# Reordering the start, the sums of x and the last half of a linear attention and SiLU kernel

## Chip, core and metric

The kernel runs on one core of a Trainium2 chip. The metric is the device time of one launch in microseconds (us); lower is better. A core has five engines with a queue each: TensorE (PE, matmuls; its weight loads are shown as PEld), VectorE (DVE), ScalarE (ACT), GpSimd (POOL) and SyncE (SP), which here only issues DMAs. Each works through its own queue, and they wait for each other by semaphores. Matmuls write into banks of PSUM; the other engines read these out.

## What is computed

Attention with a decaying state, followed by a two-layer network with SiLU:

```python
# q, k, v, alpha: (4 batch, 8 heads, 768, 48), float32
for t in range(S):
    state = alpha[:, :, t, :, None] * state + einsum('bhd,bhe->bhde', k[:, :, t], v[:, :, t])
    y[:, :, t] = einsum('bhd,bhde->bhe', q[:, :, t], state)
x = y.transpose(0, 2, 1, 3).reshape(3072, 384)
h = x @ w_in                        # (384, 2048)
g = h * (1.0 / (1.0 + exp(-h)))
out = g @ w_out                     # (2048, 384)
```

## The kernel before, in words

**Attention.** The 768 positions are cut into 6 chunks of 128, which with 4 batches makes 24 chunks `n`. A chunk goes through stages: `products` (transposes alpha, k and q, scans alpha forward and backward, and gives kp and qp), `scores` (kp times qp into two banks; ACT copies them into a tile `g`, POOL masks the part above the diagonal; then kp is transposed into `kn`), `values` (g times v, and the old state times qp: this is y, copied into `xt`) and `states` (kn times v, added to the state). The early chunks (until `settle()`) use this form, later ones one in which DVE transposes and which isn't touched. Up to here the scores tile of the attention is one single tile, `decayed`, so that chunk 1's scores can be written only when chunk 0's `values` have read it.

**Order of the stages.** The main loop counts `step`; in each step it runs up to four slots. A slot names a stage and a lag, and chunk `step - lag` is taken. An early step runs scores of the chunk before, products of the present one, then values and states of the chunk before. In step 1 the first two slots change places.

**The two-layer network.** Four chunks make a group of 512 tokens (`grp` 0 to 5), two chunks a half of 256. Work is cut into pieces, in one list `pieces`, of (generator, cost 12, the chunk from which on it may run). After each slot, `fill` runs as many pieces as are due by an even spread of their costs over the steps of a phase; what is left comes after the main loop.

- Groups 0 and 1 enter the network by `enter_plain`: four pieces of twelve matmuls (128 x 256 columns) for each half and half of w_in, and ACT's SiLU (line 909) into a tile of `gpool`, which has six buffers.
- Groups 2 to 5 use a fast matrix product with fewer products, but sums of blocks of x and of w_in. `sums_x(grp)` makes eleven such sums on DVE (lines 582 to 587) in a tile `xc`, before the group's first piece. `enter(grp, pair)` is seven pieces for half of w_in: products of 4 matmuls each (256 columns) in three banks `ps_m`, combined into the eight quarters `s[0]` to `s[7]` by ACT copies and DVE additions (line 944 and 587); SiLU in place on ACT (line 941); at the end of the seventh piece two additions `side_by_side` (line 1019) for the output product.
- `leave(grp, h)` is seven pieces for one half, 16 matmuls of 192 columns each, in two banks `ps_o`, with differences of g (`subtract`, line 1033) and with DVE or ACT putting the result in `o` (line 1042), from where it is stored by a DMA. A new product in a bank waits until `o` or `u` has been read out of it.
- `both(x, y)` takes pieces of two lists in turn. For groups 2 to 5, group `grp` enters while the group before leaves: `leave` h = 0 with `enter` pair 0, then `leave` h = 1 with `enter` pair 1, each time the leave piece first.

**Audits.** `audit()` reads alpha, w_in and w_out a second time, in blocks through one buffer `bits`, and reduces each block on DVE (line 685): a single reduce for a block of alpha, two (largest and smallest) for a block of the weights, to test that the inputs are in the range for which the fast form holds. With one buffer, SP can issue the next block's DMA only when DVE has read the last one. The main loop takes an audit every second slot; a loop after it takes the remaining ones with one or two pieces after each, and then come a few small reduces (lines 1228 to 1231) and a single matmul with their result.

**Weights at the start.** w_in arrives as doubled words and is converted on DVE in pieces of 512 columns (lines 645 to 647), between the stages of the first chunks.

Of the kernel before, what the change touches and what calls it, by code (L numbers as in the profile page):

```python
# [8 lines left out]
F32 = mybir.dt.float32  # L9
# [10 lines left out]
def general(  # L20
# [322 lines left out]
SUMS_X = (  # L343
    (9, 1, 2, 1, 4), (6, 1, 0, 1, 2), (7, 1, 2, 1, 3), (8, 1, 0, 1, 7), (10, -1, 1, -1, 8),
    (11, 1, 5, -1, 10), (12, 1, 4, 1, 11), (15, -1, 0, 1, 12), (16, 1, 1, -1, 15),
    (13, 1, 4, 1, 7), (14, -1, 6, 1, 11),
)
# [8 lines left out]
def quotients(  # L356
# [22 lines left out]
    late = {}  # L379
# [15 lines left out]
    C = 128  # L395
    NCH = S // C
    NP = H // 2
# [7 lines left out]
    GB = 4  # L405
    NG = NT // GB
    HF = NFT // 2
    NQ = NFT // 4
    TB = GB * C // 2
    HO = HD // 2  # L410

    def pool(name, bufs=1, space=None):
        kw = {} if space is None else {"space": space}
        return ctx.enter_context(tc.tile_pool(name=name, bufs=bufs, **kw))
# [5 lines left out]
    work = pool("work")  # L420
    xtp = pool("xtp", 4)
    gpool = pool("gpool", 6)
# [12 lines left out]
    def ps_attn(n=C):  # L435
        return ps_a.tile([128, 512], F32, name="ps_a").rearrange("p (j c) -> p j c", c=n)
# [59 lines left out]
    def load_v(n):  # L496
        c = ctxs.setdefault(n, dict(zip(("ci", "b"), divmod(n, B))))
        x = v[c["b"], :, c["ci"] * C : c["ci"] * C + C, :].transpose([1, 0, 2])
        t = c["v"] = vns[n % NV]
        if n < NA:  # L500
            nc.sync.dma_start(t[:, :, 0:D], x)
            return
        nc.sync.dma_start(t[:, 0 : H // 2, 0:D], x[:, 0 : H // 2])
        for e in range(2):
            nc.sync.dma_start(t[CH * e : CH * e + CH, H // 2 :, 0:D], x[CH - CH * e : C - CH * e, H // 2 :])
# [46 lines left out]
    decayed = fix.tile([128, 2 * NP * C], F32, name="g")  # L552
# [27 lines left out]
    def combine(to, sa, a, sb, b):  # L580
        if sa == sb == 1:
            return dve.tensor_tensor(to, a, b, ALU.add)
        if sa == 1:
            return dve.tensor_tensor(to, a, b, ALU.subtract)
        if sb == 1:
            return dve.tensor_tensor(to, b, a, ALU.subtract)  # L586
        return dve.scalar_tensor_tensor(to, a, -1.0, b, ALU.mult, ALU.subtract)
# [100 lines left out]
    xts, xcs = {}, {}  # L688
# [91 lines left out]
    def scores(n):  # L780
        c = ctxs[n]
        ci, b = c["ci"], c["b"]
        ps = [ps_attn() for _ in range(2)]

        for j in (0, 2, 1, 3):
            for e in range(2 if n >= NA else 1):
                for u in range(2):
                    r = slice(64 * u, 64 * u + D)  # L790
                    at = slice(CH * e, CH * e + CH) if n >= NA else slice(0, C)
                    t = slice(CH * (e ^ j // 2) if n >= NA else 0, C)
                    pe.matmul(ps[u][at, j, t], lhsT=c["kp"][r, j, at], rhs=c["qp"][r, j, t],
                              start=True, stop=True)
        g = decayed.rearrange("p (u j c) -> p u j c", u=2, j=NP)
        swapped = decayed.rearrange("p (o u j c) -> p o u j c", o=2, u=2, j=NP // 2)
        c["g"] = (lambda u, j: g[:, u, j, :]) if n < NA else (
            lambda u, j: swapped[:, j // 2, u, j % 2, :])
        for u in range(2 if n < NA else 0):
            act.copy(g[:, u], ps[u])  # L800
            gps.affine_select(g[:, u], g[:, u], pattern=[[0, NP], [1, C]], compare_op=ALU.is_ge,  # L801
                              fill=0.0, base=0, channel_multiplier=-1)
        if n >= NA:
            ps = [x.rearrange("p (o j) c -> p o j c", o=2) for x in ps]
            for u in range(2):
                act.copy(swapped[:, :, u, :, CH:], ps[u][:, :, :, CH:])  # L806
            for r, o in earlier:
                for u in range(2):
                    act.copy(swapped[r, o, u, :, 0:CH], ps[u][r, o, :, 0:CH])
            for at, half in ((CH, later), (0, earlier)):  # L810
                for r, o in half:
                    x = swapped[r, o].rearrange("p u j c -> p (u j) c")[:, :, at : at + CH]
                    gps.affine_select(x, x, pattern=[[0, NP], [1, CH]],  # L813
                                      compare_op=ALU.is_ge, fill=0.0, base=0, channel_multiplier=-1)
        if n < NA and ci < NCH - 1:
            ps_k = ps_attn()
            for j in range(NP):
                pe.transpose(ps_k[:, j, :], c["kp"][:, j, :], ident)
            c["kn"] = work.tile([128, NP, C], F32, name="kn")
            act.copy(c["kn"], ps_k)  # L820
        if ci > 0:
            s = st[b].rearrange("p j u e -> p j (u e)")
            for j in range(NP):
                mul = act.mul(s[:, j], s[:, j], least[:, n, j : j + 1])
                if late:
                    tc.keep_in_program_order(mul)
# [45 lines left out]
    def block_x(grp, at):  # L872

        if at < 2 * NKT:
            return xts[2 * grp + at % 2][:, at // 2, :]
        return xcs[grp][:, at - 2 * NKT, :]

    def sums_x(grp):
        xcs[grp] = late["xc"].tile([128, len(SUMS_X), TB], F32, name="xc")
        for to, sa, a, sb, b in SUMS_X:  # L880
            tc.keep_in_program_order(
                combine(block_x(grp, to), sa, block_x(grp, a), sb, block_x(grp, b)))
        yield
# [8 lines left out]
    turn = [0, 1, 2]  # L892
# [217 lines left out]
    def group(grp):  # L1110
        return [[(enter(grp, pair), 12, GB * grp + GB)] * 7 for pair in range(2)]

    def output(grp):
        return [[(leave(grp, h), 12, GB * grp + GB)] * 7 for h in range(2)]

    def both(x, y):
        for i in range(max(len(x), len(y))):
            pieces.extend(x[i : i + 1] + y[i : i + 1])

    pieces = []  # L1120
# [4 lines left out]
    phases = [len(pieces)]  # L1125
# [2 lines left out]
    phases.append(len(pieces))  # L1128
    before = output(1)
    for grp in range(2, NG):  # L1130
        pieces.append((sums_x(grp), 0, GB * grp + GB))
        for x, y in zip(before, group(grp)):
            both(x, y)
        phases.append(len(pieces))
        before = output(grp)
    pieces += before[0] + before[1]
# [17 lines left out]
    def settle():  # L1154

        first.close()
        late.update(look=pool("look"), part=pool("part"), xc=pool("xc"), turn=pool("turn"),
                    wx=pool("wx").tile([128, 8, NQ, 128], F32, name="wx"))
        quads = pool("quads")
        late["p"] = pool("p").tile([128, NP * W + 1], F32, name="p")  # L1160
        late["quads"] = {name: quads.tile([128, 32 + 4 * NP * D], F32, name=f"{name}t") for name in "akq"}
        for name, t in late["quads"].items():
            gps.memset(t, 1.0 if name == "a" else 0.0)
        load(NA)
# [20 lines left out]
    for step in range(STEPS):  # L1185
        if step == 1:
            load(NIN)
        stages = [[(scores, 1)], [(products, 0)], [(values, 1)], [(states, 1)]]
        if step == 1:

            stages = stages[1::-1] + stages[2:]
        elif step >= NA:
            stages = [[(land, 1), (scores, 1)], [(products, 0)], [(quotient, 0)],
                      [(values, 1), (states, 1), (flip, 0)]]
        for slot, group in enumerate(stages):
            for stage, lag in group:
                n = step - lag
                if not 0 <= n < NT:
                    continue
                stage(n)  # L1200
                if stage is values:
                    bridged = n + 1
                if stage is states and n + 1 + NIN < NA:
                    load(n + 1 + NIN)
                if stage is states and n + NV < NT:
                    load_v(n + NV)
            if step * SLOTS + slot == (NA + 1) * SLOTS - 1:
                x = decayed.rearrange("p (o i c) -> p o i c", o=2, c=C)
                for r, o in later:
                    gps.memset(x[r, o, :, 0:CH], 0.0)  # L1210
            fill(step, slot)
            if step * SLOTS + slot >= NA * SLOTS - 1 and conv_done[1] == NFT and not late:
                settle()
# [85 lines left out]
```

## Time and profile before

| | |
|---|---|
| median of 3 runs | 559.94 us (559.90 to 559.98) |
| span of the profiled execution | 558.1 us |
| what lies around the span (difference) | 1.84 us |
| VectorE idle for audit DMAs of w_out (line 685) | 19.6 us |
| audit reduces on VectorE (line 685) | 65, 42.5 us |
| additions `side_by_side` and silu in the last half | 0.68 and 1.06 us each |

The profile is one execution. Its page lists each engine's busy time, the span in 40 slices with the granted TensorE clock (9 is full speed), and groups of instructions. The answers of the trace that follow are the waits of an engine (who was waited for, at which line, in total, how often, and the longest) and the timeline: start in us, length in us, engine, line of the code, operation, result <- operands with their shapes, how many were joined in one line, and in brackets the idle time ahead and who ended it. Lengths of matmuls overlap; the distance from start to start counts.

### The profile page before, as it was taken

The numbers are of one execution on the slowest core, as the hardware profiler recorded it, in microseconds if no ns is written. First come the engines' busy times: TensorE is split into PE (matmuls) and PEld (weight loads), VectorE is DVE, ScalarE is ACT, GpSimd is POOL, SyncE is SP. The second block draws the span as 40 slices with busy tenths as digits, with TensorE's granted clock in tenths as the row PEclk, the third lists the DMA queues.
The fourth block names the chain that finished last, engine by engine and source line by source line (L and its number), as shares of the span: only waits on it lengthen the run. The fifth ranks groups of instructions, "written<-read, shape, count | busy, mean of one in ns | idle before, by whom it ended". The sixth has DMA issues, their size and how long they took to land. (4 is left out here: it accounts for less than half of the span.)

```text
span 558.1 us, 12640 instructions
## 1 busy us (share of the span) xinstructions
PE 541.4 (97%) x5026; PEld 488.8 (88%) x5026; DVE 445.1 (80%) x801; ACT 208.4 (37%) x466; POOL 75.9 (14%) x146
## 2 busy tenths in 40 slices
PE   5999999999999999999999999999999999999996
PEld 3788887998899898899999999988998999998996
DVE  5887889974999799997998986998894775857531
ACT  3456643223333243353353353353263341432200
POOL 4100010221211211021021021021121000001000
PEclk9799999999999999999999999999999999999999
DMA  9999861164445525355445654717712122333101
GB/s 218 255 276 177 232 189 40 38 164 108 126 131 136 142 62 134 88 145 157 129 109 142 194 141 115 198 22 179 180 48 84 53 99 95 111 109 106 38 25 32
DMA packets 99220, 70.13 MB, mean 126 GB/s; under 512 B 56272, under 2 KB 88656, under 8 KB 99152
## 3 DMA queue, kind: packets, MB, share of 16 engines
q1 hardware_dynamic: 97232, 65.30, 44.6%
q0 software_dynamic: 1920, 3.93, 2.0%
q8 instruction: 41, 0.67, 0.5%
q14 instruction: 27, 0.22, 0.1%
HBM read 61.34 MB, written 7.86 MB: 124 GB/s over the span
## 5 line engine op out<-in xcount | busy, mean ns | idle before, releaser
L388 PE MATMUL ps_o<-w_out,g 128*128 128x192 f32 x768 | 134.7, 329 | 1.1 <-DVE o L1042 0.9
L388 PEld LDWEIGHTS ps_o<-w_out,g 128*128 128x128 f32 x768 | 125.4, 190 | 5.1 <-DVE o L1042 2.3
L388 PE MATMUL ps_m<-xt,w_in 128*128 128x256 f32 x480 | 113.6, 383 | 1.5 <-ACT xt L851 1.1
L388 PEld LDWEIGHTS ps_m<-xt,w_in 128*128 128x128 f32 x480 | 89.1, 190 | 14.4 <-ACT xt L851 1.6
L388 PE MATMUL ps_o<-wt,g 128*128 128x192 f32 x576 | 99.7, 326 | 0.0
L388 PEld LDWEIGHTS ps_o<-wt,g 128*128 128x128 f32 x576 | 95.1, 190 | 1.6 <-issue 0.2
L388 PE MATMUL ps_m<-xc,w_in 128*128 128x256 f32 x288 | 70.7, 382 | 0.0
L685 DVE TENSOR_REDUCE seen<-bits 128x1 f32<-128x384 int32 (+2 forms) x65 | 42.5, 689 | 24.0 <-DMA bits<-in_moe_w_out_dram 19.6
L388 PEld LDWEIGHTS ps_m<-xc,w_in 128*128 128x128 f32 x288 | 53.6, 190 | 7.0 <-DVE g L944 0.3
L941 ACT ACTIVATE g<-g 128x1024 f32<-128x1024 f32 x32 | 33.0, 1056 | 59.0 <-DVE g L944 59.0
L1033 DVE TENSOR_TENSOR g<-g 128x512 f32<-128x512 f32 x72 | 49.8, 708 | 6.1 <-PE ps_o L388 6.1
L1045 POOL DMA_DIRECT2D out_dram<-o x40 | 22.0, 550 | 223.2 <-DVE o L1042 127.6
L813 POOL TENSOR_SCALAR_AFFINE_SELECT g<-g 64x256 f32<-64x256 f32 x64 | 34.2, 534 | 124.8 <-ACT g L806 105.8
L388 PE MATMUL ps_m<-xc,wx 128*128 128x256 f32 x192 | 50.0, 383 | 1.0 <-DVE xc L586 1.0
L936 ACT COPY g<-ps_m 128x512 f32<-128x512 f32 x64 | 36.5, 588 | 36.5 <-PE ps_m L388 36.4
L388 PEld LDWEIGHTS ps_m<-xc,wx 128*128 128x128 f32 x192 | 35.2, 190 | 5.3 <-ACT u L1064 1.3
L944 DVE TENSOR_TENSOR g<-ps_m,g 128x512 f32<-128x512 f32 x56 | 37.0, 684 | 2.9 <-PE ps_m L388 2.7
L722 DVE TENSOR_TENSOR_SCAN u<-al,one 128x516 f32<-128x516 f32 x24 | 30.0, 1249 | 10.6 <-ACT al L719 10.3
L909 ACT ACTIVATE g<-ps_m 128x512 f32<-128x512 f32 x32 | 19.1, 596 | 42.8 <-PE ps_m L388 42.3
L936 ACT COPY part<-ps_m 128x512 f32<-128x512 f32 x32 | 18.9, 589 | 43.0 <-DVE g L944 21.3
L752 DVE TENSOR_TENSOR_SCAN p<-al,inv 128x516 f32<-128x516 f32 x24 | 29.9, 1246 | 1.0 <-PE ps_a L388 0.4
L388 PE MATMUL ps_a<-g,vn 128*32 128x128 f32 x768 | 27.5, 278 | 1.8 <-POOL g L801 1.7
(126 smaller groups left out, 611.4 us busy)
## 6 DMA issues: line engine op xcount, KB each, us to landing
bits<-in_moe_w_in_dram SPq DMA_DIRECT2D x24, 512.0 KB, 4.8
bits<-in_moe_w_out_dram SPq DMA_DIRECT2D x32, 384.0 KB, 3.1
at<-in_alpha_dram SPq DMA_DIRECT2D x64, 96.0 KB, 2.5
kt<-in_k_dram SPq DMA_DIRECT2D x64, 96.0 KB, 2.5
qt<-in_q_dram SPq DMA_DIRECT2D x64, 96.0 KB, 2.6
bits<-in_alpha_dram SPq DMA_DIRECT2D x9, 512.0 KB, 3.8
out_dram<-o POOLq DMA_DIRECT2D x40, 96.0 KB, 2.4
flips<-turn SPq DMA_DIRECT2D x12, 256.0 KB, 2.4
```

The source lines that it names most:

```text
L388: in_order(nc.tensor.matmul(*args, **kw))
L685: dve.tensor_reduce(seen[kind][which][:, i : i + 1], x, axis=AX, op=op, apply_absolute_value=True))
L722: dve.tensor_tensor_scan(u[:, end - 1 :: -1], sg[:, end:0:-1], one[:, end:0:-1], 0.0, ALU.mult, ALU.add)
L752: dve.tensor_tensor_scan(p[:, 0:end], sg[:, 0:end], iv[:, 0:end], 0.0, ALU.mult, ALU.add)
L813: gps.affine_select(x, x, pattern=[[0, NP], [1, CH]], compare_op=ALU.is_ge, fill=0.0, base=0, channel_multiplier=-1)
L909: act.activation(gts[grp, h, pair][:, i : i + 2, q % 2, :], ps, AF.Silu)
L936: act.copy(to, ps)
L941: act.activation(x, x, AF.Silu)
L944: dve.tensor_tensor(to, a, b, op)
L1033: dve.tensor_tensor(cells(grp, h, pair, *to), cells(grp, h, pair, *x), cells(grp, h, pair, *y), ALU.subtract)
L1045: (gps if grp < NG - 1 else nc.sync).dma_start(out[r : r + C, c * HO : (c + 1) * HO], o)
```

## The change

It has three parts.

1. **Start.** Before, step 1 ran `products` of chunk 1, then `scores`, `values` and `states` of chunk 0, and step 2 `scores` of chunk 1, `products` of chunk 2, then `values` and `states` of chunk 1. Now `scores` of chunk 1 stand in step 1, between the `scores` and the `values` of chunk 0; and in step 2 `values` of chunk 1 come ahead of `products` of chunk 2. Chunk 1's scores therefore can't use the tile that chunk 0's are still in: they, and chunk 1's `kn`, are put in a tile of `gpool` that is not used yet.
2. **Sums of x.** `xc` is one tile for all groups. `sums_x` stops after the first two sums, which need only the first half of the group, and these two are put two pieces ahead of the end of the phase before.
3. **Last half.** For the last group's second pair, `enter` pieces stand ahead of `leave` pieces.

```diff
@@ scores(n)
-        g = decayed.rearrange("p (u j c) -> p u j c", u=2, j=NP)
+        if n == 1:
+
+            room = gpool.tile([128, 4, 2, TB], F32, name="g").rearrange("p a b n -> p (a b n)")
+        g = (room[:, 0 : 2 * NP * C] if n == 1 else decayed).rearrange(
+            "p (u j c) -> p u j c", u=2, j=NP)
...
-            c["kn"] = work.tile([128, NP, C], F32, name="kn")
+            c["kn"] = room[:, 2 * NP * C :][:, 0 : NP * C].rearrange(
+                "p (j c) -> p j c", j=NP) if n == 1 else work.tile([128, NP, C], F32, name="kn")
@@ sums_x(grp)
-        xcs[grp] = late["xc"].tile([128, len(SUMS_X), TB], F32, name="xc")
-        for to, sa, a, sb, b in SUMS_X:
+        xcs[grp] = late["xc"]
+        for i, (to, sa, a, sb, b) in enumerate(SUMS_X):
+            if i == 2:
+                yield
@@ the list of pieces
-        pieces.append((sums_x(grp), 0, GB * grp + GB))
-        for x, y in zip(before, group(grp)):
-            both(x, y)
+        sums = sums_x(grp)
+        pieces.insert(len(pieces) - 2, (sums, 0, GB * grp + 2))
+        phases[-1] += 1
+        pieces.append((sums, 0, GB * grp + GB))
+        for pair, (x, y) in enumerate(zip(before, group(grp))):
+            both(*((y, x) if grp == NG - 1 and pair == 1 else (x, y)))
@@ settle()
-        late.update(look=pool("look"), part=pool("part"), xc=pool("xc"), turn=pool("turn"),
+        late.update(look=pool("look"), part=pool("part"), turn=pool("turn"),
+                    xc=pool("xc").tile([128, len(SUMS_X), TB], F32, name="xc"),
@@ the main loop
-            stages = stages[1::-1] + stages[2:]
+            stages = [[(products, 0)], [(scores, 1)], [(scores, 0), (values, 1)], [(states, 1)]]
+        elif step == 2:
+            stages = [[], [(values, 1)], [(products, 0)], [(states, 1)]]
```

## The prediction

> **What bounds the kernel now.** I read the page first, then the waits of PE, the waits of DVE, the timeline at the places where these waits lie, and windows over the same stretches.
>
> ```profile
> PE 541.4 (97%) x5026; PEld 488.8 (88%) x5026; DVE 445.1 (80%) x801; ACT 208.4 (37%) x466; POOL 75.9 (14%) x146
> ...
> PEclk9799999999999999999999999999999999999999
> ```
>
> TensorE is busy for 97% of the span. Because pipelined matmuls overlap, I measure stalls as start-to-start time above the usual cadence: in the timeline 12 matmuls of 256 columns take 2.6 us (0.216 each) and 16 of 192 columns take 2.6 us (0.163 each). Only gaps above that can be won without removing matmuls, and the change removes none. The clock line has one dip, in the second slice. The waits of PE give the gaps their owners:
>
> ```profile
> PE ps_a L392 <- DMA an<-in_alpha_dram: 4.0, 1, 4.0
> PE ps_a L388 <- POOL g L801: 1.7, 1, 1.7
> PE ps_m L388 <- DVE g L944: 1.3, 2, 0.9
> PE ps_m L388 <- ACT xt L851: 1.1, 4, 0.3
> PE ps_m L388 <- DVE xc L586: 1.0, 1, 1.0
> PE ps_o L388 <- DVE o L1042: 0.9, 2, 0.7
> ```
>
> The 4.0 is the first load, which nothing here touches. The others are the whole prize: 1.7 near the start, 1.3 in group 2, 1.0 in group 4, 0.9 in the last half. So each part of the change is judged by the wait at its own place.
>
> [...] in steps of the granted clock it is half from 15.40 to 22.23 us, 6.83 us [...], after the idle of 12.2 to 13.8. [...] in the last half, additions whose operands are ready stand behind a reduce that waits for a DMA. [...]
>
> **Part A, the start (step 1 and 2).** Timelines of PE and DVE:
>
> ```profile
> 13.45 0.69 DVE L758 TENSOR_TENSOR p<-ps_m,p 128x512 f32<-128x512 f32 x1
> ...
> 20.94 1.23 DVE L722 TENSOR_TENSOR_SCAN u<-al,one 128x516 f32<-128x516 f32 x1 [0.75 <-ACT al L719]
> ...
> 33.47 0.69 DVE L647 CUSTOM_DVE_ANT_0 w_in<-w_in,up 128x1024 uint16<-128x1024 uint16 x1 [1.72 <-ACT up L629]
> ```
> ```profile
> 13.83 0.41 PE L388 MATMUL ps_a<-g,vn 128*32 128x128 f32 x4 [1.66 <-POOL g L801]
> ...
> 31.63 2.76 PE L388 MATMUL ps_m<-xt,w_in 128*128 128x256 f32 x12
> ```
>
> The same instructions are issued; SP's and POOL's queues keep their order, and no DMA moves. Chunk 1's scores go ahead of chunk 0's y. But they need p of chunk 1, which ends at 13.45 + 0.69 = 14.14, so the idle time before 13.83 is not filled: PE begins again at about 14.2. From there at half clock, with the durations seen: scores 1.2 (to 15.4), transposes of kp 0.9 (16.3), y of 0 1.7 (18.0), states 1.0 (19.0), y of 1 1.7 (20.7; its mask on POOL ends about 18.05), transposes of alpha, k, q of chunk 2, 2.2 (22.9). The first twelve matmuls on w_in then start at 22.9 and not 24.27: 1.37 gained. But chunk 2's alpha reaches ACT and DVE 1.5 later (scan at 22.45, not 20.94), and DVE has only the three w_in conversions before it that it had already. So its later conversions move by 1.46, and the sixth ends at 32.15 and not 30.69. The third group of twelve needs that sixth piece at its third matmul, which ran at 32.5; it now runs at 32.2. So 0.3 of the 1.37 survives. DVE's own wait of 1.72 before 33.47 swallows the rest of its lateness. A = −0.3. [...]
>
> **Part B, sums of x.** Eleven sums either way; two of them (0.34 us apiece from start to start) go about two pieces earlier. The kept tile adds a wait: the two first sums of a group may not overwrite blocks that the previous group still reads. These are readers of the piece before last or earlier, so it costs nothing.
>
> ```profile
> 188.43 0.69 DVE L1019 TENSOR_TENSOR g<-g 128x512 f32<-128x512 f32 x1 [2.49 <-ACT g L909]
> ...
> 190.39 1.05 DVE L582 TENSOR_TENSOR xc<-xt 128x256 f32<-128x256 f32 x3
> ```
> ```profile
> 219.37 1.13 PE L388 MATMUL ps_m<-xt,wx 128*128 128x256 f32 x4 [0.92 <-DVE g L944]
> ...
> 230.72 1.13 PE L388 MATMUL ps_m<-xt,w_in 128*128 128x256 f32 x4 [0.41 <-DVE g L944]
> ```
>
> Group 2: the two sums land before a transpose at 182.9, and the rest of that work moves into the idle 2.49 before 188.43. From 188.43 to past 232 DVE has no idle worth a wait, and it is DVE that PE waits for at 219 and 230 (gaps of 1.08 and 0.76 above cadence). All of that stretch moves up by 0.68, so the first gap shrinks by 0.68, and the second keeps its size: −0.68 once, taken as −0.7. Group 3: no wait of PE before or after. Group 4: the wait of 1.0 on xc at 369.8 stays, because DVE is without a gap from 348 to 373, between old and new place; a sum moved inside a full stretch moves nothing: 0. Group 5: two sums go ahead of a pair of audit reduces, which delays the next audit load by about 0.3; its price is in C. B = −0.7, bounds −0.9 and 0 (the scheduler also sets a state addition and weight sums later).
>
> **Part C, the last half.** The seven enter pieces now each stand ahead of a leave piece, not behind it; same matmuls, same stores. The wait that this shifts:
>
> ```profile
> 505.72 1.01 DVE L685 TENSOR_REDUCE seen<-bits 128x1 f32<-128x384 int32 x2 [2.46 <-DMA bits<-in_moe_w_out_dram]
> ...
> 509.64 1.01 DVE L685 TENSOR_REDUCE seen<-bits 128x1 f32<-128x384 int32 x2 [0.91 <-DMA bits<-in_moe_w_out_dram]
> ...
> 513.75 1.00 DVE L685 TENSOR_REDUCE seen<-bits 128x1 f32<-128x384 int32 x2
> 514.67 0.68 DVE L587 SCALAR_TENSOR_TENSOR g<-g 128x512 f32<-128x512 f32 x1
> 515.27 0.35 DVE L1042 TENSOR_TENSOR o<-ps_o,u 128x192 f32<-128x192 f32 x1
> ```
> ```profile
> 515.68 3.25 PE L388 MATMUL ps_o<-w_out,g 128*128 128x192 f32 x16 [0.71 <-DVE o L1042]
> ```
>
> One audit load is issued only when the pair of reduces before it is done: a pair every 4.0 us, 1.0 of reducing and 3.0 of landing, from 452.9 to the end. This clock doesn't care about PE. The first leave product of the last group starts at 515.68 because its bank is freed by the addition at 515.27; its excess is 0.87, and 0.28 more inside it for the last g. After the change, enter's last products come 2.6 us earlier, but on DVE the last two additions for g (into s[0] and s[3] of `enter`) still stand behind the same audit pair, which lands at 513.5 and, with B's 0.3, starts at 513.9. Then: pair ends 514.9; first addition 0.65 (515.5); silu on ACT 1.06 and hand-over 0.2 (516.75); the side-by-side addition 0.66 (517.4), which in the new order stands ahead of the bank-freeing addition of the last enter-time leave product, 0.36 (517.75). The next leave product starts at about 517.8, against 515.68 + 0.28 = 515.96 effective: +1.84. Earlier, the join at 478 to 481 loses a 0.23 gap and adds up to 0.35 of bank wait: 0. C = +1.8. Bounds: −0.5, if additions and side-by-side work finish before that audit pair; +3, if the pair comes a further microsecond late. Behind the waiting addition stand the second side-by-side addition, the last audit pair and its final checks (needed only by the one matmul at 526.7); none ends later than PE's own queue. The tail of seven and then seven more products, 2.6 each, is unchanged.
>
> **Sum.** 558.1 − 0.3 − 0.7 + 1.8 = 558.9. The runs' median, 559.94, is 1.84 above the profiled span, so I add 1.84: 560.74, forecast **560.8 us**. No-change is what lies within 0.2% (1.12 us) of 559.94: 558.82 to 561.06.
>
> **Rivals.** (1) *Audits don't hold it* (0.18): the last additions reach DVE before the audit pair, PE's gap of 0.87 + 0.28 shrinks to the 0.35 of the like place at 534.85. For it: PE delivers the operands 2.6 us sooner. Against: order in DVE's queue. 558.1 − 1.0 − 1.0 + 1.84 = **557.9 us**. (2) *The audit chain lengthens* (0.20), slower: fifteen loads hang on each other from 452.9 to 513.75; each landing 0.1 us later adds 1.5 us at the same addition, since PE is tied to the last but one pair. It decides from 0.02 us per link on, which fills the 0.26 left to the border. For it: periods in the trace differ from 3.77 to 4.18. Against: same transfers, and differences average out. 560.8 + 1.5 = **562.3 us**. (3) *All parts hidden* (0.10): DVE is full elsewhere, so B's gain is given back, A's too, and C costs less than half a microsecond: **559.9 us**. My own case has 0.52; its range is 559.7 to 561.9, so 0.30 of it lies within no change and 0.22 in slower. Of (1), 0.14 is faster and 0.04 is no change; (2) is slower; (3) no change. With my own case's remainder: faster 0.14, same 0.44, slower 0.42. The range for 8 in 10 reaches from 558.4 (most of (1) is left out) to 562.6 (A and C at their upper ends together are left out).
>
> **What would show it.** A: the first twelve w_in matmuls about 23, the third group still held to about 32.2; the clock half for 6.8 us. B: the gap before 219 down to about 0.3, that at 369 still 1.0. C: the last group's first leave product waits 1.8 to 2 us longer, for an o addition that follows a side-by-side addition and an audit pair near 513.9 less A and B. Wrong if that pair comes after those additions, if the clock dips elsewhere, or if PE shows new waits between 240 and 478.

## The result, and the profile after

The changed kernel takes 563.14 us (median of 20 runs, 559.46 to 567.31) where the kernel before takes 560.34 (20 runs, 559.46 to 562.16): ratio 1.0053, 95% interval 1.0040 to 1.0066, about 3.0 us slower. The forecast was 560.8 with a range up to 562.6, so it was more than 2 us short. The new runs are also much further apart, 7.9 us against 2.7.

The profiled execution has a span of 561.6 us, 3.5 more than before. The waits of PE after the change (waiter, who was waited for, total us, times, longest):

```profile
PE ps_a L392 <- POOL al L547: 4.1, 1, 4.1
PE ps_o L388 <- DVE o L1049: 2.6, 2, 2.4
PE ps_m L388 <- DVE w_in L647: 1.7, 1, 1.7
PE ps_m L388 <- DVE g L951: 1.1, 3, 0.5
PE ps_m L388 <- DVE xc L586: 1.0, 1, 1.0
```

Gone are the 1.7 for POOL's mask at the start and the long wait for g in group 2. New are 1.7 for a converted piece of w_in, and 2.4 for the addition `o` (its line is now 1049). Comparing the starts of the same matmul of the network in both traces gives the places:

| | before | after | later by |
|---|---|---|---|
| first twelve on w_in | 24.27 | 22.55 | -1.72 |
| 48 passes later | 39.23 | 39.93 | +0.70 |
| before group 2's gap at 218 | 214.72 | 215.45 | +0.73 |
| after it | 224.66 | 224.45 | -0.21 |
| `enter` pair 0 done | 472.95 | 472.66 | -0.29 |
| first leave product of the last group | 515.68 | 517.93 | +2.25 |
| the next one | 518.77 | 522.25 | +3.48 |
| last matmul | 553.17 | 556.72 | +3.55 |

So in this execution the stretch of A is worth +0.70, that of B with what follows it -0.99, and that of C +3.84. Timeline of PE after, at the start and in the last half:

```profile
22.55 2.76 PE L388 MATMUL ps_m<-xt,w_in 128*128 128x256 f32 x12
...
33.10 1.99 PE L388 MATMUL ps_m<-xt,w_in 128*128 128x256 f32 x8 [1.71 <-DVE w_in L647]
...
480.24 1.13 PE L388 MATMUL ps_m<-xc,w_in 128*128 128x256 f32 x4 [0.50 <-DVE g L951]
...
511.80 1.13 PE L388 MATMUL ps_m<-xt,w_in 128*128 128x256 f32 x4 [0.15 <-DVE g L951]
...
517.93 4.53 PE L388 MATMUL ps_o<-w_out,g 128*128 128x192 f32 x16 [2.40 <-DVE o L1049]
522.25 2.83 PE L388 MATMUL ps_o<-wt,g 128*128 128x192 f32 x16
```

and of DVE ahead of 517.93:

```profile
514.19 1.01 DVE L685 TENSOR_REDUCE seen<-bits 128x1 f32<-128x384 int32 x2 [0.58 <-DMA bits<-in_moe_w_out_dram]
515.12 1.28 DVE L951 TENSOR_TENSOR g<-ps_m,g 128x512 f32<-128x512 f32 x2
516.92 0.69 DVE L1026 TENSOR_TENSOR g<-g 128x512 f32<-128x512 f32 x1 [0.52 <-ACT g L948]
517.53 0.35 DVE L1049 TENSOR_TENSOR o<-ps_o,u 128x192 f32<-128x192 f32 x1
```

This is the chain of the forecast, step for step: audit pair, two additions, silu, side-by-side addition, addition that frees the bank. The forecast had the product at 517.8. What it had not is the length of that product: 16 passes of 192 columns take 4.32 us from start to start, where they took 3.09 before. The granted clock was at half from 518.96 to 522.37, for 3.41 us. Stretches of that length on both sides show where the clock was (columns: stretch, its length, then busy us and instructions of PE, PEld, DVE, ACT and POOL, granted clock, DMA share, GB/s):

```profile
512.14:515.55 3.41, 3.39 (x20) 3.02 (x18) 2.79 (x7) 1.06 (x1) 0.54 (x1) 1.00 0.46 142
515.55:518.96 3.41, 1.03 (x6) 1.03 (x7) 2.89 (x7) 2.00 (x2) 0.54 (x1) 1.00 0.35 115
518.96:522.37 3.41, 3.41 (x13) 3.41 (x12) 1.77 (x8) 0.00 (x0) 0.00 (x0) 0.50 0.09 29
522.37:525.78 3.41, 3.41 (x23) 3.41 (x22) 2.05 (x3) 0.64 (x2) 0.00 (x0) 1.00 0.00 0
```

A stretch of 3.41 us in which PE was busy for only 1.03 is followed by one at half clock: 13 passes where the next has 23. So in this execution the product behind the wait of 2.40 us also takes 1.23 us longer itself. The last section sets this wait beside others.

### The profile page after: what moved, and what is told of

It reads as the page before. It is cut to its first block, busy times and chain, and to the rows that moved or that the text cites. A ratio compares the mean times of both kernels' runs of the same rounds, so it can differ in the third digit from the quotient of the medians.

```text
span 561.6 us, 12633 instructions
## 1 busy us (share of the span) xinstructions
PE 544.0 (97%) x5026; PEld 491.4 (87%) x5026; DVE 446.6 (80%) x801; ACT 209.1 (37%) x466; POOL 77.0 (14%) x146
## 5 line engine op out<-in xcount | busy, mean ns | idle before, releaser
L388 PEld LDWEIGHTS ps_o<-w_out,g 128*128 128x128 f32 x768 | 126.9, 192 | 5.9 <-DVE o L1049 3.2
L388 PEld LDWEIGHTS ps_a<-p,kp 48*64 48x64 f32 (+1 forms) x640 | 21.4, 151 | 7.9 <-issue 4.8
```

The source lines that it names most:

```text
L388: in_order(nc.tensor.matmul(*args, **kw))
```

## The experiments

Sixteen kernels, each beside runs of the kernel before on the same chip. Ratios are to the kernel before; 0.1% is 0.56 us. Differences in us are worked out from the ratios; most of these have an interval of 0.6 to 1.0 us to each side, so a few tenths mean nothing.

**Each part alone.** The diffs are those of the three parts shown with the change, one at a time.

Part A alone:

> The kernel before with the start alone changed (part A). Theory 1, from the trace of the change: the third group of twelve w_in matmuls waits 1.7 us for its converted piece of w_in, because chunk 2's alpha reaches DVE 1.5 us or more later; net +0.7 us, median ratio about 1.001, and matmuls from 40 us on all stand 0.7 later. Theory 2: the 0.7 comes from where the half clock falls in that one execution; then the ratio is 1.000 or below and the wait before the third group is under 1 us.

Measured: 1.0024 (1.0010 to 1.0037), 1.3 us slower, runs from 559.89 to 565.30. The third group waits for its converted piece as theory 1 says (1.7 us), which rules out theory 2. But the +0.7 from 40 us on is not there: in this execution PE is 1.07 us ahead of before at 55 us and still 0.78 ahead at 473. It is 0.45 behind from the last group's first leave product on:

```profile
516.13 3.25 PE L388 MATMUL ps_o<-w_out,g 128*128 128x192 f32 x16 [1.25 <-DVE o L1047]
```

So neither theory holds as written. The section on the reasons comes back to this.

Part B alone:

> The kernel before with the sums of x alone changed (part B). Theory 1: PE's gap before the xt,wx matmuls of group 2 (0.92 us at 219) disappears, nothing else: about -1.0 us, ratio 0.998. Theory 2: the gap in the trace of the change went because A had delayed PE by 0.7 against DVE, not because of B: then B alone leaves a gap of 0.2 to 0.7 there.

Measured: 0.9970 (0.9958 to 0.9982), 1.7 us faster. PE in group 2, in its timeline:

```profile
217.46 1.03 PE L388 MATMUL ps_m<-xc,wx 128*128 128x256 f32 x4
218.32 1.03 PE L388 MATMUL ps_m<-xt,wx 128*128 128x256 f32 x4
...
229.48 1.13 PE L388 MATMUL ps_m<-xt,w_in 128*128 128x256 f32 x4 [0.41 <-DVE g L946]
```

The first gap is gone entirely (0.86 from start to start is cadence), the second stays at 0.41. Theory 1 is right about the place: B wins 1.2 us there. The lead, still 0.94 us at 473, is lost later in this execution, 0.61 of it at the join at 480 and 0.39 at the first leave product of the last group, which starts at 515.74 where it was 515.68. This execution took 560.34, the second slowest of 12; the median does keep a gain of 1.5 us (559.23 against 560.76).

Part C alone:

> The kernel before with the last half alone changed (part C). Theory 1: the first leave product of the last group waits about 2.4 us for an addition on DVE behind the audit pair and the side-by-side addition, and this gap drops the granted TensorE clock to half [...], which costs 1.3 to 1.7 more: +3.5 to +4 us, ratio 1.006 to 1.007. Theory 2: only the wait counts, +1.8 us, ratio 1.003, with the clock at full speed after it.

Measured: 1.0050 (1.0033 to 1.0067), 2.8 us slower. Its trace has two waits and no half clock:

```profile
512.96 1.13 PE L388 MATMUL ps_m<-xt,w_in 128*128 128x256 f32 x4 [1.64 <-DVE g L944]
513.93 2.76 PE L388 MATMUL ps_o<-wt,g 128*128 128x192 f32 x16
519.09 2.87 PE L388 MATMUL ps_o<-w_out,g 128*128 128x192 f32 x16 [2.40 <-DVE o L1042]
```

The wait of 2.40 is there again, and a second one of 1.64 in enter's seventh piece, for an addition that stands behind the audit pair before (which started at 511.29 here, 510.14 in the trace of the whole change). The next pair is late too:

```profile
515.34 1.01 DVE L685 TENSOR_REDUCE seen<-bits 128x1 f32<-128x384 int32 x2 [0.58 <-DMA bits<-in_moe_w_out_dram]
```

Two stretches of this run, around the second wait and behind it:

```profile
515.55:518.96 3.41, 1.14 (x8) 0.84 (x6) 2.89 (x6) 1.97 (x2) 0.04 (x1) 1.00 0.52 142
518.96:522.37 3.41, 3.28 (x20) 3.28 (x21) 3.26 (x11) 0.35 (x2) 0.54 (x1) 1.00 0.09 31
```

The wait is the same 2.40 us, and the stretch around it has nearly as little PE work as the one in the trace of the change (1.14 us against 1.03), but here the clock stays at 1.00. The 2.8 us lie between theory 2 (+1.8) and theory 1 (+3.5 to +4), and neither is right for this execution: without any half clock C loses 3.5 us in it (0.50 ahead of before at 473, 3.03 behind at the last matmul), as the audit pair came 1.6 us later than before.

**Filling the gap.** Matmuls whose result nobody reads (fillers), ahead of the last group's first leave product, in the whole change:

```diff
         a, b = new(0), new(1)
+        if 2 * grp + h == 2 * NG - 2:
+            idle = ps_a.tile([128, 512], F32, name="ps_a")[:, 0:256]
+            for _ in range(10):
+                pe.matmul(idle, lhsT=w_in[:, 0, 0:128], rhs=w_in[:, 0, 0:256],
+                          start=True, stop=True)
```

> The changed kernel with ten matmuls of 256 columns added just ahead of the last group's first leave product, whose result nobody reads (2.2 us of PE work in the 2.4 us gap). Theory 1 (the gap halves the clock): the product starts when it did, 517.9 or up to 0.2 later, its 16 matmuls take 2.6 us and not 4.3, the time falls by 1.5 to 1.7 us against the change. Theory 2 (its slow matmuls wait for operands, each 0.32 us apart): no gain, or a loss of up to 0.3.

Measured: 1.0084 (1.0057 to 1.0111), worse. The trace shows 20 passes, 4.3 us of work for a gap of 2.4, so its total says nothing on the theory. With five (`range(5)`):

> The changed kernel with half the earlier filling ahead of the last group's first leave product: the trace of the earlier one shows that its ten matmuls ran as twenty passes of 0.216 us, 4.3 us and not 2.2, so they overfilled the gap. Five take 2.2 us. If a gap of 2.4 us there is what halves the clock [...], the product starts at most 0.2 us later than without them and its passes stay 0.163 us apart; the time is 0.5 to 1.7 us below the change. If not, it is the same or up to 0.3 longer.

Measured: 1.0053 (1.0038 to 1.0068), the same as the change. Its timeline:

```profile
511.71 1.13 PE L388 MATMUL ps_m<-xt,w_in 128*128 128x256 f32 x4 [1.77 <-DVE g L951]
...
515.27 2.32 PE L388 MATMUL ps_a<-w_in 128*128 128x256 f32 x10
517.89 2.87 PE L388 MATMUL ps_o<-w_out,g 128*128 128x192 f32 x16 [0.29 <-DVE o L1049]
```
In this execution the product starts when it did (517.89) and runs at full speed. That fits the theory of the clock, but the medians don't: the forecast gain of 0.5 to 1.7 us did not come. Nine of its 22 runs have a mean granted clock of 0.995 or less, ten of 20 of the change, so the drop is not gone; the unfilled gap in enter's seventh piece (1.77 here) is one place where it can come from. In the trace with ten matmuls the half clock began at 513.13, right after that gap (2.23 us there). That the filling pays is not shown.

**Audits taken earlier**, to see whether their chain holds the end:

```diff
-        if at % 2 == 0 and step > 3 * GB + 2:
+        if (at % 2 == 0 or step >= 20) and step > 3 * GB + 2:
```

> The kernel before with the audits taken in every slot, not every second, from step 20 on: ten more in the main loop, seven left for the loop after it. Theory 1 (the chain of audit loads, each issued after the pair before it, holds the last group's first leave product): its last pair comes some 30 us or more sooner, the gap of 0.87 us at 514.6 falls to 0.35 or less, -0.5 to -1.2 us. Theory 2 (banks and additions hold it): the gap stays, 0.

> Part B with the same earlier audits. Theory 1: B's gain of about 1 us in group 2, which in its own trace was gone again at the first leave product of the last group (-0.94 ahead of it, +0.06 after it), now reaches the end: -2 to -2.5 us against before. Theory 2: B's gain is lost elsewhere, no more than -1.5.

> Parts B and C with the earlier audits. Theory 1: with no audit ahead of the last additions on DVE, C costs nothing: within 0.5 us of B with early audits, gap ahead of the last group's first leave product at most 0.5 us, no half clock there. Theory 2 (C's order is bad in itself, by silu, side-by-side addition and the bank): it stays 1.5 us or more slower than B with early audits.

Measured: 1.0209 (1.0188 to 1.0231), 1.0157 (1.0132 to 1.0182) and 1.0178 (1.0156 to 1.0200). All forecasts of the total failed: the added audits stand in DVE's queue just where it is full. In the first of the three, group 4's sums of x start behind an audit pair that waits 2.0 us for its load, at 374.88 and not at 362.40. The waits of PE there:

```profile
PE ps_m L388 <- DVE xc L582: 11.6, 1, 11.6
```

The mean granted clock of this execution is 0.989, that of the profiled one of before 0.994. What can be read is the end alone: without B as well as with it, early audits let the last group's first leave product follow without a wait (with B 530.28 + 0.86 = 531.14), and with C added the wait there is 0.45 us, not 2.40. That speaks for the chain, but a cleaner test was needed.

**Audit loads that don't hang on each other.** By the end the buffers of k and q are free. The sixteen loads of w_out take them and the audit's own in turn, two loads ahead of the reduces:

```diff
-        for src, n, kind in todo:
-            t = late["look"].tile([128, 512, 2], I32, name="bits")
+        own, loads = len(todo) - NFT, []
+        for k, (_, _, kind) in enumerate(todo):
+            while len(loads) < (min(len(todo), k + 3) if k >= own else k + 1):
+                m = len(loads)
+                src, n, sort = todo[m]
+                if m < own or (m - own) % 3 == 0:
+                    t = late["look"].tile([128, 512, 2], I32, name="bits")
+                else:
+                    t = late["quads"]["kq"[(m - own) % 3 - 1]][:, 0 : 2 * HD].bitcast(I32).rearrange(
+                        "p (n w) -> p n w", w=2)
...
+                loads.append(x)
+            x = loads[k]
             yield
```

> The kernel before, where the sixteen audit loads of w_out (all at the end) take three buffers in turn, the audit's own and the two in which k and q came, free by then; two loads are under way while one block is reduced. Order of DVE and PE otherwise as before. Theory 1 (each audit load waits for the pair before it, and this chain sets when the last group's leave starts): DVE's wait for w_out audits falls from 19.6 us to under 3, the gap of 0.87 us ahead of the last group's first leave product to under 0.4, -0.5 to -1 us. Theory 2 (banks and additions): no change.

> Part B with three buffers for the audit loads. Theory 1: B's gain reaches the end and the gap at the last leave goes as well: -2 to -3 us against before. Theory 2: no more than B alone, -1.7.

> Parts B and C with three buffers for the audit loads. Theory 1: C, 2.8 us dearer alone, costs nothing here or gains up to 0.8 (the gap at the last leave at most 0.4, the products of enter's seventh piece don't wait for DVE), so -2 to -3.5 us against before. Theory 2 (C's order itself is bad, because silu and the side-by-side addition stand ahead of the addition that frees the bank): at least 1.5 us slower than B with three buffers.

> The whole change with three buffers for the audit loads. Theory 1: what is left of the change's cost is A's: 0 to 1.3 us slower than B and C with three buffers, so about -1 to -2.5 us against before, with runs still a few us apart at the start. Theory 2: still at or above before.

| | ratio | 95% interval | median, us | runs, us |
|---|---|---|---|---|
| before, three buffers | 0.9960 | 0.9946 to 0.9975 | 558.62 | 557.33 to 559.14 |
| B, three buffers | 0.9927 | 0.9914 to 0.9939 | 556.46 | 556.12 to 557.42 |
| B and C, three buffers | 0.9949 | 0.9935 to 0.9962 | 557.94 | 557.01 to 558.54 |
| A, B and C, three buffers | 0.9974 | 0.9965 to 0.9984 | 558.93 | 557.20 to 559.72 |

Theory 1 holds for the first two, and by more than it said: DVE's wait for w_out audits is down from 19.6 us,

```profile
DVE seen L696 <- DMA bits<-in_moe_w_out_dram: 1.3, 1, 1.3
```

(this line stands in the waits of DVE of both), and the last group's first leave product follows without a gap. B gains 1.8 us on top of the buffers (0.9927 against 0.9960), about what it gains alone (1.7): in the medians the two add up. C costs 1.2 us on top of B (0.9949 against 0.9927), neither nothing nor as much as theory 2 asked. PE and DVE in the trace of B and C:

```profile
514.80 2.87 PE L388 MATMUL ps_o<-w_out,g 128*128 128x192 f32 x16 [1.36 <-DVE o L1055]
```
```profile
511.83 0.69 DVE L1032 TENSOR_TENSOR g<-g 128x512 f32<-128x512 f32 x1 [0.26 <-ACT g L954]
512.78 0.69 DVE L1032 TENSOR_TENSOR g<-g 128x512 f32<-128x512 f32 x1 [0.26 <-ACT g L954]
513.39 1.00 DVE L696 TENSOR_REDUCE seen<-bits 128x1 f32<-128x384 int32 x2
514.31 0.17 DVE L1245 TENSOR_REDUCE ends<-seen 128x1 f32<-128x28 f32 x1
514.40 0.35 DVE L1055 TENSOR_TENSOR o<-ps_o,u 128x192 f32<-128x192 f32 x1
```

No load is waited for here any more, but the last pair of reduces, 1.0 us, stands in the queue ahead of the addition that frees the bank. The last two runs of this group take that away too, by ending the audits sooner:

```diff
-        for _ in range(1 + turns % 2):
-            go_on()
+        go_on()
```

> Parts B and C with three buffers, and one piece of work after each audit in the last loop, not one and two in turn: the last audit is over before enter's seventh piece. Theory 1 (the 1.36 us gap left with B and C is the last pair of reduces, 1.0 us, ahead of the addition that frees the bank): the gap falls to 0.4 or less, 1 to 1.4 us below B and C with three buffers. Theory 2 (silu and side-by-side additions hold it): the gap stays over 1 us.

> Part B with three buffers and one piece after each audit: the other half of the comparison. Theory 1: the 0.4 us of slow passes in the last group's first leave product stay, the rest is as B with three buffers, within 0.5 us of it; so C then gains 0 to 0.5 us. Theory 2: over 0.5 us from it.

Measured: B and C 0.9963 (0.9950 to 0.9976), B 0.9957 (0.9944 to 0.9970). The wait falls almost as forecast, from 1.36 to 0.45:

```profile
514.38 2.87 PE L388 MATMUL ps_o<-w_out,g 128*128 128x192 f32 x16 [0.45 <-DVE o L1055]
```

and C is now 0.3 us dearer than B, within the intervals. But the forecasts of the total failed: B and C gained nothing over their run with one and two pieces (0.9963 against 0.9949), and B alone lost 1.7 us (0.9957 against 0.9927). The trace of B with faster audits does not show that loss (counted from 100 us on, it is within 0.2 us of the other), so why is open.

**Part A without the noise of the chain:**

> Parts A and B with three buffers for the audit loads: against B with three buffers alone this is A by itself without the noise of the audit chain. Theory 1: A costs 0.7 to 1.5 us in the median, its runs 2 us or more apart (B's were 1.3 apart), because the third group of w_in matmuls waits for its converted piece when the clock is half at the start and doesn't when it is full. Theory 2: A's cost was an effect of the audit chain: then within 0.5 us of B with three buffers.

Measured: 0.9956 (0.9940 to 0.9971), runs from 556.33 to 560.33. A costs 1.6 us over B with three buffers, much as alone (1.3) and on top of B and C (1.4). So A's cost does not come from the one-buffer chain. The reason in theory 1 fails, though: the third group waits 1.7 us in all six traces with A's order, with full clock at 12.9 us already (the change with five fillers, where four 128x128 transposes take 0.66 us there) as with full clock from 20.6. And the runs fall in two groups: the eight with a mean clock of 0.998 or more have a median of 556.87, 0.4 above B with three buffers, the five with 0.995 or less one of 559.86. The next run moves one stage back:

```diff
-            stages = [[], [(values, 1)], [(products, 0)], [(states, 1)]]
+            stages = [[], [(products, 0)], [(values, 1)], [(states, 1)]]
```

> As the run of A and B with three buffers, with one stage moved back: in step 2 chunk 2's products come ahead of chunk 1's values. Theory 1 (A's cost is that chunk 2's alpha reaches DVE 1.5 us later, and the w_in conversions with it): the conversions come 1.0 to 1.5 us sooner, the wait for the converted piece is gone, 0.7 to 1.5 us below A and B with three buffers. Theory 2 (something else at the start costs): no change.

Measured: 0.9949 (0.9936 to 0.9963). The wait for the converted piece is down from 1.7 to 0.5 us in its trace, but the two intervals overlap, and its execution had the clock at full speed from 10.3 us on, the other from 20.6. Less of A's cost comes back than forecast, 0.4 us and not 0.7 to 1.5.

## Why the prediction failed

| part | forecast, us | alone | with three buffers |
|---|---|---|---|
| A | -0.3 | +1.3 | +1.6 over B, +1.4 over B and C |
| B | -0.7 | -1.7 | -1.8 |
| C | +1.8 | +2.8 | +1.2 over B |
| sum of the parts | +0.8 | +2.4 | |
| whole change | +0.8 | +3.0 | +0.8 over before with three buffers |

Two terms failed, A's and C's: A in its sign, by 1.6 us, and C in its size, by 1.0 alone and by 2.0 in the profiled execution. B erred by 1.0 the other way and hid a part of this. The +0.8 in the last cell is luck: it is the forecast's sum with other parts.

**A, forecast -0.3, measured +1.3 to +1.6.** The mechanism was seen: the first twelve matmuls come 1.7 us sooner in the profiled execution, alpha of chunk 2 later (scan at 22.77; forecast 22.45), and the third group waits for its converted piece. The forecast had the piece ready at 32.15; it was at 33.04, as ACT and DVE were late by some tenths more. So the step "0.3 of the 1.37 survives" failed: nothing does. The other part of it is the premise that the clock at the start is fixed. Full clock was granted from very different times in different executions (in the trace of the change four 128x128 transposes take 1.11 us at 16.42 and 0.66 at 21.18; in that of before they take 1.12 at 7.54 and 0.63 at 8.83), and the position at 55 us against before goes with it:

| full clock from, us | without A | with A |
|---|---|---|
| 10 to 13 | -0.76, -1.23, -1.30, -1.43 | -0.88, -1.07, -1.34 |
| 16 to 19 | -0.71, -0.47, -0.02, +0.19, +0.24 | +0.24 |
| 20.6 | none seen | +0.70, +0.79 |
| 8.6 to 8.9, then half for a time (15.40 to 22.23 in before) | 0 (before), +0.24 | none seen |

With an early clock A gains nothing that the old order hasn't as well; with a late one it is behind. These are single profiled executions, so the table supports this but does not isolate it, and at equal clock it shows at most some tenths of A's 1.3 us. In the runs of A and B with three buffers most of the cost lies in the five with a low mean clock; in those of A, B and C only one of nine is low, so that is not the whole cause. A candidate for such drops, not shown, is the wait of 1.7 us itself: in the trace of the change full clock stays on behind it, but in that of before a wait of 1.66 us is followed by half clock (last section).

**B, forecast -0.7, measured -1.7 alone.** The place was right (the first gap in group 2, the second kept, nothing in groups 3 and 4: the wait of 1.0 for xc is there after as before). The size was too small: the addition that PE waits for came 1.24 us sooner (217.38, before 218.62) and not 0.68. From 180 us to that addition DVE runs the same instructions in both; its idle time before 188.4 shrank by 0.87, and the other 0.37 lies in their order and length (the scan just ahead took 1.23 us, not 1.49). Two readings of the prediction are off without effect here: the second gap is 0.68 above cadence, not 0.76, and the longest period of the audits in the trace of before is 4.29 us, not 4.18.

**C, forecast +1.8, measured +2.8 alone and +3.84 in the profiled execution.** The kind was right, and so was the order on DVE that makes the wait. How well shows when the product is counted from the start of the audit pair ahead of it:

| trace | audit pair | first leave product | distance |
|---|---|---|---|
| before | 513.75 | 515.68 | 1.93 |
| A alone | 514.20 | 516.13 | 1.93 |
| B alone | 513.81 | 515.74 | 1.93 |
| the change | 514.19 | 517.93 | 3.74 |
| C alone | 515.34 | 519.09 | 3.75 |
| the change, five fillers | 514.14 | 517.89 | 3.75 |

C adds 1.8 us between pair and product, as forecast, in each of these three traces. What the sum "C = +1.8" had wrong is the rest. First, the time of the pair was set at 0.15 later than before; it came 0.44 later in the trace of the change and 1.59 later with C alone. Second, a lead that PE has does not move a product that waits for the pair: the 0.29 us that A and B had gained by 473 are lost there in the trace of the change. Third, the half clock was put at nothing: 4.32 us for the product instead of 3.09, +1.23 here. With 1.81 for the order these make 3.77 of the 3.84. Two more waits lie before the product and cost nothing by themselves, since it waits for the pair anyway: at the join at 478 to 481, taken as 0, the gap is 0.66 above cadence (0.23 before), and enter's seventh piece waits for the audit pair before, 0.3 us above cadence in the trace of the change, 1.8 with C alone.

**The rival about the audit chain.** The slower rival, a lengthening chain of audit loads, had the right object: the pair ahead of the product started at 513.8 before, 514.2 after, and 515.3 and 515.1 in two others with C (C alone, ten fillers). Whether C itself makes it late is not shown: with A alone it came at 514.2 too, and the periods of one trace differ by half a microsecond. Taking the chain away is worth 2.2 us by itself (0.9960), turns C from +2.8 alone to +1.2 on top of B, and with B makes the fastest version measured, 0.9927 or 4.1 us below before. On the whole change it is worth more, 4.4 us (0.9974 against 1.0053).

**Spread.** Ten of the change's 20 runs have a mean clock of 0.995 or less, with a median of 564.6 us; the other ten, at 0.997 or more, 562.3. So even those are 2 us above before, and the clock carries only a part of the loss. With B and C on three buffers no run is below 0.998, and the runs are 1.5 us apart. That fits the waits of C behind the chain as what drops the clock in the last half; but a mean does not say where the clock fell, and A's start adds its own spread (five of 13 runs of A and B with three buffers are at 0.995 or less).

**Left open.** Why one piece after each audit is slower, what carries A's cost, why the audit pair came late in some traces, and how often each of C's gaps drops the clock.

## What to carry to other kernels

When work is moved ahead on one engine, look for a chain with a period of its own that its operands pass: here a buffer of one, so that every load waits for the reduces of the last. In the six traces compared, the product queued behind that chain starts at a fixed distance from its pair (1.93 us without C, 3.74 to 3.75 with C), and a lead ahead of it does not move that product; the medians show that such a lead is not always lost (B gains as much with the chain as without). Freeing the chain (two idle buffers) gained 2 us by itself, and 4 together with the one part of the change that closes a real gap. And a forecast wait on TensorE of some 2 us is not priced by its length alone: in the trace of the change the product behind a wait of 2.40 us ran at half clock and took 4.32 us, not 3.09; with C alone the clock stayed at full speed behind a wait of the same length.

## What the hardware showed that was not expected

- Half clock followed some waits of PE and not others of like length. In each row the stretch ends where the clock fell, or lies around the wait where it did not fall:

| trace | wait of PE, us | stretch of 3.4 us | PE busy in it, us | granted clock in the 3.4 us after it |
|---|---|---|---|---|
| before | 1.66 (to 13.83) | 11.99 to 15.40 | 1.65 | 0.50 |
| the change | 1.71 (to 33.10) | 30.85 to 34.27 | 1.71 | 1.00 |
| the change | 2.40 (to 517.93) | 515.55 to 518.96 | 1.03 | 0.50 |
| C alone | 2.40 (to 519.09) | 515.55 to 518.96 | 1.14 | 1.00 |
| the change, ten fillers | 2.23 (to 512.93) | 509.72 to 513.13 | 1.18 | 0.50 |
| the change, five fillers | 1.77 (to 511.71) | 508.73 to 512.14 | 1.64 | 1.00 |

The second row, from its trace:

```profile
30.85:34.27 3.42, 1.71 (x7) 1.19 (x8) 3.08 (x6) 2.02 (x4) 1.65 (x2) 1.00 0.81 216
34.27:37.68 3.41, 3.41 (x23) 3.12 (x22) 3.24 (x6) 1.65 (x3) 0.00 (x0) 1.00 0.84 218
```

- So neither the length of a wait nor the work in the stretch around it tells by itself whether the clock fell: 1.14 us of work was followed by full clock, 1.65 by half.
- The time from which full clock is granted at the start varied from 8.6 to 20.6 us between executions, and two executions fell back once (15.40 to 22.23 in before, 6.83 us; in that of B and C with three buffers and faster audits four 128x128 transposes take 0.66 us at 11.67, 1.11 at 18.28 and 0.66 again at 22.90).
- In the execution with PE's wait of 11.6 us (early audits, without B) the mean granted clock was 0.989; the two other runs with early audits were profiled at 0.988 (B) and 0.989 (B and C).
